# Preparing the second FFN's weights in step with the first FFN, and partly inside the second

## The chip, the cores and the metric

One core of one Trainium2 chip runs the kernel alone. The metric is the time of one execution on the device in microseconds (us). Engines: PE (TensorE, matmuls), DVE (VectorE), ACT (ScalarE), POOL (GpSimd); SP issues every DMA.

## What is computed

```python
# attention: batch 4, 8 heads, 576 tokens, head size 64, causal window of 128, a linear bias per head
x = attention(q, k, v)                       # 2304 tokens x 512
h = x @ w_in                                 # first FFN, 512 -> 2048
x = (h * sigmoid(1.702 * h)) @ w_out         # 2048 -> 512
g = x @ w_gate                               # second FFN, 512 -> 1536
v = x @ w_val
out = (g * sigmoid(g) * v) @ w_out           # 1536 -> 512, with a w_out of its own
```

All inputs are fp32. The second FFN's three weights arrive in DRAM as 64-bit words.

## The kernel before

**Tiling.** The 18 tiles of 128 tokens are split into five blocks of 4, 2, 4, 4 and 4 tiles (0 to 4). A *step* of the first FFN is one pair (block, 128 of the 2048 hidden columns): `h_steps` does 12 matmuls into a PSUM bank `hp`, ACT's `th<-hp` (tanh), DVE's `th<-th,hp`, ACT's `gh<-th` and DVE's `gl<-th,gh` (the high and the low part of the activation). `y_part` then adds 12 matmuls from `gh` and `gl` into four `y` banks. `y_part` runs two steps behind `h_part` (`AHEAD`). There are 80 steps in the order: block 0, steps 0 to 7; block 1; block 0's other eight (its *second half*); blocks 2, 3 and 4. The eight PSUM banks are one ring, so a late reader of a bank holds up the PE, which runs its instructions in order, as every engine does.

**Attention** of blocks 2, 3 and 4 is put between the steps of the blocks ahead of them: block 2's lies beside block 1 and block 0's second half, block 3's beside block 2, block 4's beside block 3. Nothing of attention lies beside block 4. It uses banks `sb` (scores), `pt` (transposes) and `xb` (values). At the end of a block the four `y` banks are evicted through one SBUF buffer `yt` to DRAM; block 0's second half first loads its earlier sum (`part`), into one of the two `th` buffers.

**Preparation of the second FFN's weights.** It works in *units*. A unit loads `raw` (512 KB), turns the words into fp32 `cs` (ACT `cs<-raw`, then three DVE operations, the last `cs<-cs,raw`), and splits that into a high part (ACT) and a low part (POOL), which SP writes to a scratch in DRAM. 24 units are for gate and value (G, V): they also make four sums `cs<-cs` on DVE, and their parts are `wa`, `wa` and `wb`. 12 units are for the output weight (O), with the part `wo`. The generators `prepare_gv` and `prepare_o` yield after each piece, 8 pieces for a G or V unit and 5 for an O unit; `advance` traces the next pieces. Before, `PACE` traces 6 pieces in each step from block 2 on, whatever is left of G and V ahead of block 4, and the O units in block 4.

**What sets the order.** The hand-written `PLAN` covers the start only. Behind it a scheduler orders all that is traced, at compile time: an instruction stands on its engine's queue where its inputs and buffers are ready by the scheduler's reckoning, so work that is traced late may stand early.

**Second FFN.** Three superblocks of six tiles, six weight pairs each: 18 turns `q`. A turn is 14 products of 6 matmuls (banks `sx`, `sy`, `sz`), four gates, and six output parts. Its inputs `ya` are built by `y_steps` (ACT and POOL), its weights `wg` and `wo` are loaded from the scratch each turn.

Of the kernel before, what the change touches and what calls it, by code (L numbers as in the profile page):

```python
# [16 lines left out]
P = 128  # L17
# [6 lines left out]

PACE = 3, 3

O_SLOTS = 4

SUPER = 6
# [44 lines left out]
def attention_two_ffn(ctx: ExitStack, tc: tile.TileContext, q, k, v, w_in, w_out, w_gate, w_val, w_out2, yscr, wscr, woscr, out):  # L74
# [149 lines left out]
    def flat(t):  # L224
        return t.bitcast(F32).rearrange("p s r c -> p (s r c)")

    def fetch_gv(pool, p, m, h):
        raw = pool.tile([P, 2, 2, P, 2], U32, tag="er", name="raw")
# [4 lines left out]
        return raw  # L233

    def prepare_gv(pool, raw, fetch_next, p, m, h):
# [24 lines left out]
        nc.sync.dma_start(out=at[:, 2048 + h * 768 : 2048 + (h + 1) * 768], in_=flat(wb))  # L260
        yield

    def prepare_o(pool, tag, f):
        raw = pool.tile([P, 512, 2], U32, tag=tag(), name="raw")
        nc.sync.dma_start(
            out=raw.rearrange("p c w -> p (c w)"), in_=w_out2[f * P : (f + 1) * P, :].bitcast(U32)
        )
        yield
        cs = cvp.tile([P, 8, P], F32, tag="cv", name="cs")
        yield from fraction(raw, cs)  # L270
        t = pool.tile([P, 1, 2, 512], F32R, tag=tag(), name="wo")
        halves(t, slice(0, 1), cs.rearrange("p s c -> p (s c)")[:, :512].unsqueeze(1))
        nc.sync.dma_start(out=woscr[f // 2][:, f % 2 * 1024 : (f % 2 + 1) * 1024], in_=flat(t))
        yield
# [277 lines left out]


    xs = {}
    ys = {}
    gs = {}

    def h_steps(j, f):
# [17 lines left out]
        gl = gp.tile([P, TMAX * P], F32R, tag="gl", name="gl")  # L576
        nc.scalar.activation(out=gh[:, :m], in_=th[:, :m], func=AF.Copy)  # L577
        yield
        nc.vector.tensor_tensor(out=gl[:, :m], in0=th[:, :m], in1=gh[:, :m].bitcast(F32), op=ALU.subtract)  # L579
        gs[j, f] = (gh, gl)  # L580
# [43 lines left out]
    def y_steps(s, tile_of):  # L624
# [15 lines left out]
        def minus(out_, a, b):  # L640
            nc.gpsimd.tensor_tensor(out=out_, in0=a, in1=b, op=ALU.subtract)

# [47 lines left out]
    def gv_steps(q):  # L690
# [212 lines left out]
    bctx = ExitStack()  # L903
    gv_todo = [(p, m, h) for p in range(NP2) for m in "GV" for h in range(2)]
    o_todo = list(range(NF2))

    def gv_work():
        raws = []

        def fetch_next():  # L910
            if len(raws) < len(gv_todo):
                raws.append(fetch_gv(att, *gv_todo[len(raws)]))

        fetch_next()
        yield
        for i, u in enumerate(gv_todo):
            yield from prepare_gv(att, raws[i], fetch_next, *u)

    turn = [0]

    def o_tag():
        turn[0] += 1
        return f"w{(turn[0] - 1) % O_SLOTS}"

    def o_work():
        for f in o_todo:
            yield from prepare_o(wpool, o_tag, f)

    gv_work, o_work = gv_work(), o_work()

    def advance(work, n):
        for _ in range(n):
            next(work, None)

    for idx, (j, f) in enumerate(seq):
# [4 lines left out]
        if j < 2:  # L940
# [17 lines left out]
        if j >= 2:  # L958
            advance(gv_work, PACE[1])
        if j == na - 1:  # L960
            if f % 2:
                next(first, None)
            if f >= O_SLOTS + 2:
                advance(o_work, 6)
    for i in range(len(seq) - AHEAD, len(seq)):
# [9 lines left out]
    for q in range(NQ):  # L975
# [71 lines left out]
```

## Time and profile before

| | |
|---|---|
| median of 3 runs | 961.38 us (961.23 to 965.03) |
| profiled execution | 959.06 us |
| its span | 957.3 us |
| PE busy | 925.3 us (97%) |
| DVE, ACT, POOL busy | 594.1, 423.7, 340.0 us |

The span is the time from the first to the last instruction of the profiled execution, 1.8 us less than its own time. A busy PE is not a PE at its peak, because the end of a matmul is modelled; starts are exact.

### The profile page before, as it was taken

How to read it: one execution, taken by the hardware profiler on the slowest of the kernel's cores; microseconds unless marked ns; L12 is line 12 of the kernel's file. 1: busy time of each engine (PE TensorE's matmuls, PEld its weight loads, DVE VectorE, ACT ScalarE, POOL GpSimd, SP SyncE). 2: the span in 40 equal slices, each digit the busy share in tenths (PEclk: the TensorE clock that was granted, in tenths of full speed). 3: DMA queues.
4: the chain of work that ended last, by engine and by line, in shares of the span. 5: the costliest groups of instructions: out<-in, count | busy, mean ns of one | idle time of the engine just before them, and what ended most of it. 6: DMA issues, size and time to landing. Idle time of an engine off the chain costs nothing.

```text
span 957.3 us, 15271 instructions
## 1 busy us (share of the span) xinstructions
PE 925.3 (97%) x5464; PEld 791.9 (83%) x5464; DVE 594.1 (62%) x1369; ACT 423.7 (44%) x968; POOL 340.0 (36%) x410
## 2 busy tenths in 40 slices
PE   7799999988999999999999999999999999999998
PEld 5477897776777777788887899999999999999997
DVE  7997898877777775433477474556534444535455
ACT  5664566655555454433345353234343333242331
POOL 4734007654466343313534461117511111111121
PEclk8899999999999999999999999999999999999999
DMA  9953204667556551010669385665775667766641
GB/s 335 346 210 124 76 2 156 217 227 248 209 183 229 202 213 52 15 50 1 198 206 360 123 301 201 210 219 202 263 243 205 212 215 245 252 213 208 216 166 66
DMA packets 62476, 182.40 MB, mean 191 GB/s; under 512 B 6080, under 2 KB 28096, under 8 KB 55488
## 3 DMA queue, kind: packets, MB, share of 16 engines
q1 hardware_dynamic: 62400, 181.43, 54.7%
q8 instruction: 43, 0.70, 0.3%
q14 instruction: 33, 0.27, 0.1%
HBM read 142.61 MB, written 38.80 MB: 189 GB/s over the span
## 4 chain that ended last, share of the span: by engine, by line
PE 61%; DVE 14%; DMA 10%; ACT 5%; issue 5%; POOL 4%; SPq 1%; DVEq 0%; POOLq 0%; ACTq 0%
PE o L751 16%; PE sx L681 15%; PE sz L681 8%; PE sy L681 4%; DMA raw<-in_moe_w_out 3%; PE y L549 3%; PE y L550 3%; PE y L551 3%; PE hp L549 2%; PE hp L551 2%; PE hp L550 2%; DVE cs L215 2%; DVE raw L211 2%; DMA wraw<-in_moe_w_out 2%; DMA y_scratch<-yt 2%
## 5 line engine op out<-in xcount | busy, mean ns | idle before, releaser
L715 POOL TENSOR_TENSOR p<-th,p 128x384 fp32r<-128x384 f32 x72 | 74.0, 1028 | 282.1 <-PE sz L681 147.8
L681 PE MATMUL sx<-ya,wg 128*128 128x384 f32 x864 | 173.3, 336 | 0.7 <-ACT pc L697 0.7
L751 PE MATMUL o<-wo,p 128*128 128x512 f32 x648 | 159.6, 391 | 0.0
L681 PEld LDWEIGHTS sx<-ya,wg 128*128 128x128 f32 x864 | 153.2, 188 | 6.5 <-ACT pc L697 1.0
L751 PEld LDWEIGHTS o<-wo,p 128*128 128x128 f32 x648 | 120.7, 188 | 21.3
L549 PE MATMUL hp<-xh,wt 128*128 128x512 f32 (+1 forms) x320 | 122.4, 382 | 4.7 <-DVE th L571 3.2
L550 PE MATMUL y<-gl,wt 128*128 128x512 f32 (+1 forms) x320 | 117.6, 373 | 2.3 <-DVE gl L579 2.3
L551 PE MATMUL hp<-xh,wt 128*128 128x512 f32 (+1 forms) x320 | 118.6, 371 | 0.0
L550 PE MATMUL hp<-xl,wt 128*128 128x512 f32 (+1 forms) x320 | 118.4, 370 | 0.0
L551 PE MATMUL y<-gh,wt 128*128 128x512 f32 (+1 forms) x320 | 117.2, 372 | 0.0
L549 PE MATMUL y<-gh,wt 128*128 128x512 f32 (+1 forms) x320 | 112.1, 381 | 4.8 <-DVE yt L611 2.9
L409 POOL TENSOR_SCALAR prob<-prob,stat 128x128 f32<-128x128 f32 x144 | 68.5, 495 | 128.4 <-DVE sb L319 56.8
L760 DVE SCALAR_TENSOR_TENSOR acc<-o,acc 128x512 f32<-128x512 f32 x90 | 61.9, 689 | 46.0 <-PE o L751 44.1
L681 PE MATMUL sz<-ya,wg 128*128 128x384 f32 x432 | 84.1, 335 | 0.0
L579 DVE TENSOR_TENSOR gl<-th,gh 128x512 fp32r<-128x512 f32 (+1 forms) x80 | 61.7, 776 | 32.8 <-ACT gh L577 32.8
L702 DVE TENSOR_TENSOR c<-sy,pc 128x384 f32<-128x384 f32 x36 | 20.1, 557 | 92.1 <-PE sy L681 92.1
L549 PEld LDWEIGHTS hp<-xh,wt 128*128 128x128 f32 x320 | 60.7, 190 | 19.5 <-DVE th L571 4.6
L681 PEld LDWEIGHTS sz<-ya,wg 128*128 128x128 f32 x432 | 75.8, 188 | 0.1
L549 PEld LDWEIGHTS y<-gh,wt 128*128 128x128 f32 x320 | 57.4, 189 | 19.6 <-DVE yt L611 3.3
L714 ACT ACTIVATE p<-th 128x384 fp32r<-128x384 f32 x72 | 37.5, 520 | 79.2 <-DVE th L712 79.2
L550 PEld LDWEIGHTS y<-gl,wt 128*128 128x128 f32 x320 | 60.8, 190 | 13.5 <-DVE gl L579 3.5
L551 PEld LDWEIGHTS y<-gh,wt 128*128 128x128 f32 x320 | 60.6, 189 | 11.2 <-issue 0.8
(90 smaller groups left out, 1524.7 us busy)
## 6 DMA issues: line engine op xcount, KB each, us to landing
wg<-w_scratch SPq DMA_DIRECT2D x36, 1024.0 KB, 6.6
wg<-w_scratch SPq DMA_DIRECT2D x36, 768.0 KB, 5.4
wo<-wo_scratch SPq DMA_DIRECT2D x18, 1024.0 KB, 7.0
w_scratch<-wa SPq DMA_DIRECT2D x24, 512.0 KB, 2.8
w_scratch<-wb SPq DMA_DIRECT2D x24, 384.0 KB, 2.9
wraw<-in_moe_w_in SPq DMA_DIRECT2D x16, 512.0 KB, 7.4
wraw<-in_moe_w_out SPq DMA_DIRECT2D x16, 512.0 KB, 8.6
raw<-in_moe_w_gate SPq DMA_DIRECT2D x24, 256.0 KB, 3.5
```

The costliest lines, as they stand in the source:

```text
L211: nc.vector.scalar_tensor_tensor(out=low, in0=low, scalar=29, in1=high, op0=ALU.logical_shift_right, op1=ALU.bitwise_or)
L409: (nc.vector if (j, hp, g) in NORM_ON_VECTOR else nc.gpsimd).tensor_scalar(out=prob[:, x], in0=prob[:, x], scalar1=stat[:, 3, x : x + 1], ...
L549: nc.tensor.matmul(out=out_ap, lhsT=whi, rhs=xhi, start=start, stop=False)
L550: nc.tensor.matmul(out=out_ap, lhsT=whi, rhs=xlo, start=False, stop=False)
L551: nc.tensor.matmul(out=out_ap, lhsT=wlo, rhs=xhi, start=False, stop=stop)
L579: nc.vector.tensor_tensor(out=gl[:, :m], in0=th[:, :m], in1=gh[:, :m].bitcast(F32), op=ALU.subtract)
L681: nc.tensor.matmul(out=bank_[:, :HT], lhsT=w[:, kk, at, a, :], rhs=y[:, b, kk, :], start=start and kk == 0 and n == 0, stop=kk == 1 and n ...
L702: nc.vector.tensor_tensor(out=t, in0=b[:, :HT], in1=kept[m, k], op=ALU.add)
L714: nc.scalar.activation(out=ph[:, 0, at], in_=th, func=AF.Copy)
L715: nc.gpsimd.tensor_tensor(out=ph[:, 1, at], in0=th, in1=ph[:, 0, at].bitcast(F32), op=ALU.subtract)
L751: nc.tensor.matmul(out=o, lhsT=ph[:, a, c], rhs=w[:, f, b, :], start=f == 0 and n == 0, stop=f == 1 and n == 2)
L760: nc.vector.scalar_tensor_tensor(out=acc, in0=o, scalar=0.5, in1=acc, op0=ALU.mult, op1=ALU.add)
```

## The change

Three things change. All 36 units go into one list ordered by weight pair, O units 2.5 pairs later, with the next unit's `raw` always loaded one unit ahead; the pace is 3.6 pieces a step in blocks 2 and 3, 6.8 in block 4 up to its step 13, and 0.7 for each product of the second FFN from product 6 of turn 0 on, until the list is done. Each piece's instructions are tied, in order, behind the last traced `gh` and `gl` (in the second FFN, behind the last `keep_copy` and `add`). The attention's buffers are closed at step 6 of block 4 and not at its step 0, and the first superblock's `y_steps` move there, with their four subtractions on DVE and not on POOL.

```diff
-PACE = 3, 3
+CLOSE = 6
+PACE = {2: 1.8, 3: 1.8, 4: 3.4}
+PAUSE = 13
+PACE_LATE = 0.7
 O_SLOTS = 4
+LATER = 2.5
...
+    def prepare(slot, raw, fetch_next, unit):
+
+        m, p, h = unit
         cs = cvp.tile([P, 8, P], F32, tag="cv", name="cs")
-        yield from fraction(raw.rearrange("p f a c w -> p (f a c) w"), cs)
+        yield from fraction(raw, cs)
         fetch_next()
+        if m == "O":
+            pool, tag = slot()
+            t = pool.tile([P, 1, 2, 512], F32R, tag=tag, name="wo")
+            halves(t, slice(0, 1), cs.rearrange("p s c -> p (s c)")[:, :512].unsqueeze(1))
+            nc.sync.dma_start(out=woscr[p][:, h * 1024 : (h + 1) * 1024], in_=flat(t))
+            yield
+            return
...
-            nc.gpsimd.tensor_tensor(out=out_, in0=a, in1=b, op=ALU.subtract)
+            (nc.gpsimd if s else nc.vector).tensor_tensor(out=out_, in0=a, in1=b, op=ALU.subtract)
...
+    todo = [(m, p, h) for p in range(NP2) for m in "GVO" for h in range(2)]
+    todo.sort(key=lambda u: u[1] + (LATER if u[0] == "O" else 0))
+    closed, turn = [], [0]
+
+    def slot():
+        if not closed:
+            return att, "er"
+        turn[0] += 1
+        return wpool, f"w{(turn[0] - 1) % O_SLOTS}"
...
+    def advance(n):
+        owed[0] += n
+        while owed[0] >= 1:
+            owed[0] -= 1
+            with ExitStack() as after:
+                for ins in marks.values():
+                    after.enter_context(tc.issue_after(ins))
+                next(work, None)
...
-        if (j, f) == (na - 1, 0):
-            advance(gv_work, 1000)
+        if (j, f) == (na - 1, CLOSE):
+            closed.append(True)
             attx.close()
...
-        if j >= 2:
-            advance(gv_work, PACE[0])
+        if (j, f) < (na - 1, PAUSE):
+            advance(PACE.get(j, 0))
...
         for n, (m, i) in enumerate(gv_steps(q)):
-            advance(o_work, 1)
+            if q or n > 5:
+                advance(PACE_LATE)
```

DVE in block 0's second half, between the `gl` of the 26th step and the next. Before:

```order
L579 TENSOR_TENSOR gl<-th,gh 128x512
L215 SCALAR_TENSOR_TENSOR cs<-cs,raw 128x512
L247 TENSOR_TENSOR cs<-cs 128x128 x3
L571 SCALAR_TENSOR_TENSOR th<-th,hp 128x512
L247 TENSOR_TENSOR cs<-cs 128x128
L545 TENSOR_TENSOR xb<-xb,half 128x512
L209 TENSOR_SCALAR raw<-raw 128x512
L211 SCALAR_TENSOR_TENSOR raw<-raw 128x512
L538 TENSOR_TENSOR xl<-xb,xh 128x512
L215 SCALAR_TENSOR_TENSOR cs<-cs,raw 128x512
```

The same place in the changed kernel:

```order
L592 TENSOR_TENSOR gl<-th,gh 128x512
L584 SCALAR_TENSOR_TENSOR th<-th,hp 128x512
L557 TENSOR_TENSOR xb<-xb,half 128x512
L550 TENSOR_TENSOR xl<-xb,xh 128x512
L592 TENSOR_TENSOR gl<-th,gh 128x512
```

The preparation has left this stretch. Counted by `cs<-cs,raw` on DVE's queue, units stand as follows: before block 2, 8 before and 0 now; block 2, 15 and 7; block 3, 1 and 8; block 4, 12 (all O) and 12 (8 G and V, 4 O); second FFN, 0 and 9 (3 G and V, 6 O).

SP's queue at the end of block 0's second half, where `part` is loaded and `yt` written. Before:

```order
L232 DMA raw<-in_moe_w_val 128x2x256 x2
L610 DMA part<-y_scratch 128x512
L256 DMA w_scratch<-wa 128x1024
L618 DMA y_scratch<-yt 128x512
L610 DMA part<-y_scratch 128x512
L260 DMA w_scratch<-wb 128x768
L610 DMA part<-y_scratch 128x512
```

Now:

```order
L311 DMA vr<-in_v 128x320 x4
L624 DMA part<-y_scratch 128x512
L632 DMA y_scratch<-yt 128x512
L624 DMA part<-y_scratch 128x512 x2
L308 DMA qr<-in_q 128x512
```

The unit's transfers no longer stand between the `part` loads.

ACT in turn 2 of the second FFN, whose copies `pc` and gates (`th`, `p`) stand here. Before:

```order
L697 ACTIVATE pc<-sx 128x384
L697 ACTIVATE pc<-sz 128x384
L697 ACTIVATE pc<-sx 128x384
L697 ACTIVATE pc<-sz 128x384
L710 ACTIVATE th_6088<-c_6067 128x384
L697 ACTIVATE pc<-sx 128x384 x2
L714 ACTIVATE p_6022<-th_6088 128x384
```

Now:

```order
L711 ACTIVATE pc<-sx 128x384
L229 ACTIVATE wo<-cs 128x512
L711 ACTIVATE pc<-sz 128x384
L216 ACTIVATE cs<-raw 128x512
L724 ACTIVATE th_6039<-c_6014 128x384
L711 ACTIVATE pc<-sx 128x384 x2
L216 ACTIVATE cs<-raw 128x512
L229 ACTIVATE wo<-cs 128x512
L728 ACTIVATE p_5961<-th_6039 128x384
```

Two O units' `cs<-raw` stand between the turn's copies, with one gate step and two copies between them.

## Rows read from the trace of the kernel before

**Rows 1.** Busy time of each engine in six stretches of the span.

```profile
core 0: us, PE busy (x) PEld busy (x) DVE busy (x) ACT busy (x) POOL busy (x), PEclk, DMA share, GB/s
161.20:226.30 65.10, 60.71 (x450) 47.07 (x451) 51.27 (x154) 39.49 (x104) 37.38 (x57) 0.97 0.63 217
226.30:348.60 122.30, 116.01 (x758) 89.68 (x758) 92.66 (x267) 64.58 (x170) 63.25 (x90) 0.99 0.62 213
348.60:452.60 104.00, 102.71 (x683) 80.44 (x682) 46.87 (x150) 43.64 (x112) 32.04 (x55) 1.00 0.15 49
452.60:536.60 84.00, 82.20 (x362) 67.40 (x361) 53.59 (x68) 37.56 (x63) 39.02 (x24) 1.00 0.69 238
541.00:655.00 114.00, 113.34 (x605) 106.76 (x604) 58.55 (x92) 44.79 (x90) 36.31 (x29) 1.00 0.64 222
655.00:940.00 285.00, 285.00 (x1498) 266.26 (x1497) 142.66 (x241) 95.74 (x193) 71.17 (x61) 1.00 0.63 216
```

**Rows 2.** The same stretches, line L549 alone (a third of a step's matmuls).

```profile
161.20:226.30 65.10, 28.04 (x68) 13.15 (x68) 0.97 0.63 217
226.30:348.60 122.30, 52.17 (x130) 24.54 (x130) 0.99 0.62 213
348.60:452.60 104.00, 48.73 (x121) 22.70 (x121) 1.00 0.15 49
```

**Rows 3.** The same, tile `sb` alone: PE, PEld and DVE.

```profile
161.20:226.30 65.10, 3.31 (x64) 2.06 (x64) 9.29 (x44) 0.97 0.63 217
226.30:348.60 122.30, 8.77 (x144) 5.13 (x144) 16.51 (x74) 0.99 0.62 213
348.60:452.60 104.00, 6.99 (x96) 4.08 (x96) 13.21 (x62) 1.00 0.15 49
```

**Rows 4.** The same, tile `xb` alone: PE, PEld, DVE and ACT.

```profile
161.20:226.30 65.10, 5.27 (x160) 4.21 (x160) 5.51 (x8) 4.71 (x8) 0.97 0.63 217
348.60:452.60 104.00, 7.06 (x192) 6.35 (x192) 5.57 (x8) 4.79 (x8) 1.00 0.15 49
```

**Rows 5.** The same, line L215 alone: DVE's `cs<-cs,raw`, one for each unit.

```profile
161.20:226.30 65.10, 5.36 (x8) 0.97 0.63 217
226.30:348.60 122.30, 9.71 (x15) 0.99 0.62 213
452.60:536.60 84.00, 13.40 (x12) 1.00 0.69 238
```

**Rows 6.** ACT in order of time, a step's `th<-hp` behind a unit's part.

```profile
191.45 0.42 ACT L221 ACTIVATE wa<-cs 128x256 fp32r<-128x256 f32 x1 [0.77 <-DVE cs L215]
193.40 0.58 ACT L569 ACTIVATE th<-hp 128x512 f32<-128x512 f32 x1
```

**Rows 7.** PE in order of time: the last `hp` matmul, and the next.

```profile
189.82 0.40 PE L551 MATMUL hp<-xh,wt 128*128 128x512 f32 x1
...
194.76 0.80 PE L549 MATMUL hp<-xh,wt 128*128 128x512 f32 x1 [2.58 <-DVE th L571]
```

**Rows 8.** PE's waits in the whole span: in total, times, longest.

```profile
PE y L549 <- DVE yt L611: 2.9, 1, 2.9
PE y L550 <- DVE gl L579: 2.3, 4, 0.9
...
PE y L549 <- ACT yt L615: 1.1, 1, 1.1
```

**Rows 9.** DVE in order of time: the first `yt` of block 0's second half.

```profile
230.24 0.69 DVE L611 SCALAR_TENSOR_TENSOR yt<-y,part 128x512 f32<-128x512 f32 x1 [1.55 <-DMA part<-y_scratch]
```

**Rows 10.** Tile `raw`: its transfers, from issue to landing.

```profile
DMA to landing us min/median/max: 2.9/3.6/6.5
```

**Rows 11.** DVE's `gl` in block 3, without and with POOL's `ya` beside it.

```profile
441.69 0.69 DVE L579 TENSOR_TENSOR gl<-th,gh 128x512 fp32r<-128x512 f32 x1 [2.06 <-ACT gh L577]
...
447.23 2.24 DVE L579 TENSOR_TENSOR gl<-th,gh 128x512 fp32r<-128x512 f32 x1 [2.06 <-ACT gh L577]
...
445.26 3.65 POOL L637 TENSOR_TENSOR ya<-yr,ya 128x768 fp32r<-128x768 f32 x2 [20.34 <-ACT ya L636]
```

More of the change, by code (lines that the diff above doesn't have):

```diff
@@ L225, in flat, with fetch @@
         return t.bitcast(F32).rearrange("p s r c -> p (s r c)")
-    def fetch_gv(pool, p, m, h):
-        raw = pool.tile([P, 2, 2, P, 2], U32, tag="er", name="raw")
+    def fetch(slot, unit):
+        m, p, h = unit
+        pool, tag = slot()
+        if m == "O":
+            raw = pool.tile([P, 512, 2], U32, tag=tag, name="raw")
+            src = w_out2[(2 * p + h) * P : (2 * p + h + 1) * P, :].bitcast(U32)
+            nc.sync.dma_start(out=raw.rearrange("p c w -> p (c w)"), in_=src)
+            return raw
+        raw = pool.tile([P, 2, 2, P, 2], U32, tag=tag, name="raw")
         w = w_gate if m == "G" else w_val
@@ L232, in fetch_gv @@
             nc.sync.dma_start(out=raw[:, f].rearrange("p a c w -> p a (c w)"), in_=src)
-        return raw
-    def prepare_gv(pool, raw, fetch_next, p, m, h):
+        return raw.rearrange("p f a c w -> p (f a c) w")
+    def prepare(slot, raw, fetch_next, unit):
+        m, p, h = unit
         cs = cvp.tile([P, 8, P], F32, tag="cv", name="cs")
-        yield from fraction(raw.rearrange("p f a c w -> p (f a c) w"), cs)
+        yield from fraction(raw, cs)
         fetch_next()
+        if m == "O":
+            pool, tag = slot()
+            t = pool.tile([P, 1, 2, 512], F32R, tag=tag, name="wo")
[3 more added lines that the diff above has]
+            return
         a11, a12, a21, a22, s4, s3, s1, s2 = (cs[:, i] for i in range(8))
@@ L260, in prepare_gv @@
         nc.sync.dma_start(out=at[:, 2048 + h * 768 : 2048 + (h + 1) * 768], in_=flat(wb))
[L261 to L273, printed above, removed]
         yield
@@ L551, in three @@
         nc.tensor.matmul(out=out_ap, lhsT=wlo, rhs=xhi, start=False, stop=stop)
+    marks = {}
     xs = {}
@@ L576, in h_steps @@
         gl = gp.tile([P, TMAX * P], F32R, tag="gl", name="gl")
-        nc.scalar.activation(out=gh[:, :m], in_=th[:, :m], func=AF.Copy)
+        a = nc.scalar.activation(out=gh[:, :m], in_=th[:, :m], func=AF.Copy)
         yield
-        nc.vector.tensor_tensor(out=gl[:, :m], in0=th[:, :m], in1=gh[:, :m].bitcast(F32), op=ALU.subtract)
+        d = nc.vector.tensor_tensor(out=gl[:, :m], in0=th[:, :m], in1=gh[:, :m].bitcast(F32), op=ALU.subtract)
+        marks["a"], marks["d"] = a.ins, d.ins
         gs[j, f] = (gh, gl)
@@ L696, in keep_copy @@
             t = pp.tile([P, HT], F32, tag="pc", name="pc", bufs=5)
-            nc.scalar.activation(out=t, in_=b[:, :HT], func=AF.Copy)
+            marks["a"] = nc.scalar.activation(out=t, in_=b[:, :HT], func=AF.Copy).ins
             kept[m, i] = t
@@ L701, in add @@
             t = pp.tile([P, HT], F32, tag="c2", name="c2", bufs=4)
-            nc.vector.tensor_tensor(out=t, in0=b[:, :HT], in1=kept[m, k], op=ALU.add)
+            marks["d"] = nc.vector.tensor_tensor(out=t, in0=b[:, :HT], in1=kept[m, k], op=ALU.add).ins
             c[m, i] = t
@@ L903, in attention_two_ffn, with preparation @@
     bctx = ExitStack()
-    gv_todo = [(p, m, h) for p in range(NP2) for m in "GV" for h in range(2)]
-    o_todo = list(range(NF2))
-    def gv_work():
+    todo = [(m, p, h) for p in range(NP2) for m in "GVO" for h in range(2)]
[6 more added lines that the diff above has]
+        return wpool, f"w{(turn[0] - 1) % O_SLOTS}"
+    def preparation():
         raws = []
         def fetch_next():
-            if len(raws) < len(gv_todo):
-                raws.append(fetch_gv(att, *gv_todo[len(raws)]))
+            if len(raws) < len(todo):
+                raws.append(fetch(slot, todo[len(raws)]))
         fetch_next()
         yield
[L916 to L933, printed above, removed]
+        for i, u in enumerate(todo):
+            yield from prepare(slot, raws[i], fetch_next, u)
+    work, owed = preparation(), [0.0]
+    def advance(n):
[6 more added lines that the diff above has]
+                next(work, None)
     for idx, (j, f) in enumerate(seq):
@@ L957, in attention_two_ffn @@
         run(2 * idx + 1)
[L958 to L964, printed above, removed]
+        if (j, f) < (na - 1, PAUSE):
+            advance(PACE.get(j, 0))
+        if j == na - 1 and f > CLOSE and f % 2:
+            next(first, None)
     for i in range(len(seq) - AHEAD, len(seq)):
```

3 lines of the change are left out of this document (2 added, 1 removed).

## The prediction, made before the changed kernel ran

> **What bounds the kernel now.** I read first the busy time by stretch. I cut the span where DVE's `gl` of a block's steps begin, so that the stretches are block 0's second half (65.1 us), block 2 (122.3), block 3 (104.0) and block 4 (84.0), then the first five turns of the second FFN and the rest [rows 1]. In the last stretch the PE is busy for 285.00 of 285 us, at the full granted clock: there the time is the PE's, and other engines' work is free as long as it isn't late. In block 2 the PE is busy for 116.0 of 122.3 us, while DVE is busy for 76% of it. In block 3, whose attention is of the same kind but which holds almost no units, DVE is busy for 45%.
>
> The cut is DVE's, and the PE stands now further ahead of it, now less, so the stretches don't hold the same matmuls; I take the first FFN's out by their count. Block 4 has no attention: 82.20 us for 362 matmuls is 0.227 us each [rows 1], or 0.681 us for each matmul of L549 with its two partners. That leaves for attention and stalls [rows 1, 2]:
>
> - block 0's second half: 65.1 − 68 × 0.681 = 18.8 us
> - block 2: 122.3 − 130 × 0.681 = 33.8 us
> - block 3: 104.0 − 121 × 0.681 = 21.6 us
>
> Block 2 also holds 48 more `sb` matmuls than block 3 [rows 3]; at 6.99/96 = 0.073 us each these are 3.5 us. So block 2 lost 33.8 − 21.6 − 3.5 = 8.7 us that block 3 didn't. Block 0's second half holds 64 of 96 `sb` matmuls and 160 of 192 `xb` matmuls [rows 3, 4]: by the one share it should take 14.4 us, by the other 18.0. I take the middle, 16.2, so it lost 2.6 us (0.8 to 4.4). What differs is the units: 8, 15 and 12 of them by their `cs<-cs,raw` in block 0's second half, block 2 and block 4 [rows 5], and one in block 3 by the order.
>
> How a unit costs PE time is seen in the order of time at 190 us. The last `hp` matmul starts at 189.82, so `hp` is done about 190.2 [rows 7]. ACT could take `th<-hp` then, but `wa<-cs` of a unit stands ahead of it and waits 0.77 us for DVE's `cs<-cs,raw`; `th<-hp` starts at 193.40 [rows 6]. The PE waits 2.58 us for the bank [rows 7], and the clock that the rows grant falls to 0.97 over this stretch [rows 1], which is 2.0 us of it. The waits are thus a matter of queues: a unit's piece in front of a step's piece.
>
> **Block 0's second half: −2.6 us.** The order shows no unit left there. All that its units cost comes back: 0.8 to 4.4 us.
>
> **Block 2's end of block 0: −1.5 us.** The `y` banks of block 0 leave one after another through `part`. The PE waited 2.9 us for `yt`, once [rows 8]; the first `yt` itself waited 1.55 us for `part` [rows 9]. The clock row of 0.99 is 1.2 us of block 2's 122.3 [rows 1]. Block 3 waits 1.1 us for its own `yt` [rows 8], so 2.9 + 1.2 − 1.1 = 3.0 us of the 8.7 are this chain's. In the changed queue of SP no unit's transfer stands between the `part` loads, and less is in flight beside them. But `part` still takes a `th` buffer, and still lands before `yt`. I take half: bounds 0 and −3.0 us.
>
> **Block 2: −4.3 us.** The other 8.7 − 3.0 = 5.7 us belong to 15 units: 0.38 us each. Now 7 units stand there. What one costs when fewer crowd is bounded by 0.38 above, and by block 4 below: 12 units beside steps without attention cost two waits for `gl` of 0.9 us [rows 8], 0.15 us each. Attention is still there, but at half the rate a unit's piece meets a step's piece less often; I take 0.2, so 1.4 us stay. Bounds: −3.0 (0.38 each) and −5.7 (none).
>
> **Block 3: +1.6 us.** Eight units where one was; at 0.2 us 1.6. Bounds 0 and +3.0. It has room: 15 units raised DVE's share in block 2 by 31 points over block 3's 45%, so 8 units raise block 3's to some 62 to 65%.
>
> **Block 4: 0.** Twelve units before and now; eight have four more operations on DVE, but they begin at the block's first step and not at its seventh. The `ya` splits move a few steps later, and four subtractions of 128x768 go from POOL to DVE; no row has them on DVE, so I bound them by `gl` (128x512, 0.69 us [rows 11]) below and by twice that above: 3 to 6 us in all, beside 84 us in which DVE is busy for 53.6. Bounds ±1.8 us, the two waits for `gl` gone or doubled.
>
> **Second FFN: +0.7 us.** Nine units stand in the first turns, where none was. The first 114 us already carry such work before (POOL busy for 32%, against 25% behind it, with `ya` of the next superblock) and the PE lost 114.0 − 113.3 = 0.7 us there [rows 1]. I take once more that. Bounds: 0, and the rival below.
>
> The Trainium skill (GPSIMD Engine Reference, Specifications) says that POOL shares its SBUF interfaces with VectorE and contends with DVE instructions that have two inputs in SBUF. The trace agrees: `gl` took 2.24 us beside POOL's `ya`, and 0.69 us one step earlier with POOL idle [rows 11]. This speaks against the change in the second FFN, where every unit brings POOL one to three parts beside the gates; by 1.55 us for each of nine units it would be 14 us of DVE time. DVE has half of its time free there, so I add nothing for it.
>
> **Sum.** −2.6 − 1.5 − 4.3 + 1.6 + 0 + 0.7 = −6.1 us. The profiled execution took 959.06 us (1.8 us of it outside the span), so 953.0. The median of the three runs is 961.38, higher by a factor of 1.0024; on its scale the forecast is 955 us. With every bound at its best the sum is −4.4 − 3.0 − 5.7 + 0 − 1.8 + 0 = −14.9, or 946.5 on the median's scale; at its worst without the rival below −0.8 − 0 − 3.0 + 3.0 + 1.8 + 0.7 = +1.7, or 963.
>
> **Rivals.** *The cost moves with the units.* If a unit costs 0.38 us wherever attention is, 15 units in blocks 2 and 3 cost what they did in block 2 alone: −2.6 − 3.0 + 3.0 + 0.7 = −1.9 with the `yt` chain unchanged, 957.2, and 959.5 on the median's scale. For it: the tie sets only the earliest place, and in the new order units' parts still stand ahead of `th<-hp` now and then. Against it: 8.7 us in one block and almost nothing in the next is more than in proportion to DVE's 76% and 45%.
>
> *The second FFN waits for `raw`.* ACT and DVE take their instructions in order; behind a `cs<-raw` whose transfer is late stand the copies `pc` and the sums that free the banks for the PE. For two O units in a row, the second `raw` is issued only when the first has gone through three DVE operations, some 2 us, and it lands 2.9 to 6.5 us later [rows 10]. The new order puts a gate step and two copies between the two `cs<-raw`; at 285.00/1498 = 0.19 us for a matmul [rows 1] a product is 1.14 us, so that is about 3.4 us. With the median landing of 3.6 us `cs<-raw` is 2 + 3.6 − 3.4 = 2.2 us late, with the longest 5.1. A bank is wanted again one to four products later (1.1 to 4.6 us). If it is one, six O units cost 6 × (2.2 − 1.1) = 7 us at the median landing and 24 at the longest; I take 3.3 us late, the middle of 2.2 and 4.4: 6 × 2.2 = 13 us. The sum is then −6.1 + 13 = +7, 966 and 968.5 on the median's scale. It decides from a landing of about 4.5 us on, if nothing but one product lies between. Against it: the scheduler can put work of the next product in front, and in the first five turns the PE lost only 0.7 us in all while the weights' loads and `ya` went on [rows 1].
>
> The Trainium skill (DMA: Bandwidth & Descriptors, Issuing engines are not separate DMA queues) has all transfers share the same 16 DMA engines and interleave. The share is 0.63 to 0.64 in both stretches of the second FFN [rows 1], so units there lengthen `raw` and the weights' loads; it feeds this rival and has no price of its own here.
>
> *The units cost nothing once tied.* If the tie keeps pieces out of the steps' way altogether, blocks 0, 2 and 3 give −2.6 − 3.0 − 5.7 = −11.3, plus 0.7: 948.5, and 951 on the median's scale.
>
> **Chances.** Three runs of one kernel differ by up to 0.4%, so 0.5% (4.8 us) is about what can be told from no change. Forecast, between 952 and 958: 0.48. Free once tied, below 952: 0.21. Cost moves along, 958 to 963: 0.18. Waiting for `raw`, above 963: 0.13. A gain of over 0.5% is below 956.6: all of the second case and most of the first, 0.62. No change 0.26, slower 0.12 (above 966.2, nearly all of the last case). Leaving out the last case and the best few, the range is 946 to 963; the forecast alone, with its bounds, is 950 to 959.
>
> **What would show it.** Right: no unit's operation before block 2, PEclk 1.00 in block 0's second half, no wait of the PE for `th` there; the remainder of block 2 by the reckoning above near 28 us and of block 3 near 23; DVE busy about 65% in both; the first five turns within 1 us of 114. Wrong: block 3's remainder rises by as much as block 2's falls; or `sx`, `sy` or `sz` waits for `c` or `pc` while ACT's `cs<-raw` waits for a transfer; or the 2.9 us wait for `yt` stands as before.

## The result and the profile after

The changed kernel takes 948.47 us (median of four runs, 945.89 to 949.73), the kernel before 961.31 us on the same chip (four runs). The ratio is 0.9858 with an interval of 0.9821 to 0.9894, a gain of about 13 us. The profiled execution took 945.89 us and its span is 944.2. That is inside the range of 946 to 963, but below the forecast's 955 and below the 950 to 959 that the forecast alone spans: the gain is about twice the 6.1 us that the sum gave.

Busy time of each engine after, in stretches cut as in [rows 1] where DVE's `gl` of a block's steps begin, columns as there:

```profile
159.90:214.30 54.40, 54.40 (x459) 43.57 (x453) 27.24 (x100) 25.97 (x74) 13.98 (x28) 1.00 0.18 55
214.30:322.40 108.10, 108.10 (x738) 85.51 (x737) 68.70 (x216) 52.58 (x141) 43.68 (x69) 1.00 0.42 145
322.40:431.30 108.90, 108.90 (x720) 85.37 (x719) 68.08 (x197) 52.55 (x135) 44.53 (x68) 1.00 0.36 124
431.30:521.80 90.50, 86.48 (x376) 69.81 (x375) 65.81 (x102) 42.25 (x78) 40.93 (x35) 1.00 0.74 261
521.80:640.00 118.20, 116.10 (x619) 109.10 (x619) 77.70 (x131) 54.53 (x111) 50.22 (x43) 1.00 0.83 295
```

Line L561 alone (L549 before), which holds a third of a step's matmuls, as in [rows 2]:

```profile
159.90:214.30 54.40, 24.75 (x62) 11.65 (x62) 1.00 0.18 55
214.30:322.40 108.10, 51.22 (x128) 24.16 (x129) 1.00 0.42 145
322.40:431.30 108.90, 51.02 (x128) 23.91 (x128) 1.00 0.36 124
```

In the first three stretches the PE is now busy without a gap, at the full granted clock. DVE is busy for 64% of block 2 and 63% of block 3, as the prediction had it. With 0.681 us for each L561 matmul as in the prediction, 12.2 us remain in block 0's second half (18.8 before), 20.9 in block 2 (33.8) and 21.7 in block 3 (21.6). Block 4 goes the other way: 90.5 − 123 × 0.681 = 6.7 us remain, where the 84.0 us before were its matmuls and 1.6 us. DVE's busy time and the DMA share grow in the two stretches that follow block 3.

These stretches do not hold the same matmuls on both sides. For the comparison I therefore cut at the PE itself, at the first `hp` matmul of a step, which is the same instruction in every kernel: steps 24, 32, 48, 64 and 79, counted in the order in which steps are issued. PE rows in order of time (start, duration), before:

```profile
154.07 0.48 PE L549 MATMUL hp<-xh,wt 128*128 128x512 f32 x1
...
214.89 0.39 PE L549 MATMUL hp<-xh,wt 128*128 128x512 f32 x1
...
335.02 0.40 PE L549 MATMUL hp<-xh,wt 128*128 128x512 f32 x1
...
446.36 0.39 PE L549 MATMUL hp<-xh,wt 128*128 128x512 f32 x1
...
530.37 0.39 PE L549 MATMUL hp<-xh,wt 128*128 128x512 f32 x1
```

The same five matmuls after:

```profile
154.67 0.39 PE L561 MATMUL hp<-xh,wt 128*128 128x512 f32 x1
...
206.71 0.39 PE L561 MATMUL hp<-xh,wt 128*128 128x512 f32 x1
...
314.57 0.40 PE L561 MATMUL hp<-xh,wt 128*128 128x512 f32 x1
...
424.98 0.39 PE L561 MATMUL hp<-xh,wt 128*128 128x512 f32 x1
...
511.70 0.39 PE L561 MATMUL hp<-xh,wt 128*128 128x512 f32 x1
```

Their differences give the table by stage, in us; the last stage runs to the end of the span and holds block 4's last step and the second FFN. The rows for the experiments below are read in the same way. "Units" are counted by their `cs<-cs,raw` in the instruction order of DVE, in five places: ahead of block 2, in blocks 2, 3 and 4, and in the second FFN.

```
kernel          start  0 (2nd half)  block 2  block 3  block 4  rest   span   units
before          154.1      60.8       120.1    111.3     84.0   426.9  957.3  8/15/1/12/0
after           154.7      52.0       107.9    110.4     86.7   432.5  944.2  0/7/8/12/9
after, again    155.6      52.0       107.9    110.4     87.5   434.4  947.8  0/7/8/12/9
untied          155.4      59.3       125.4    108.3     86.1   435.7  970.2  8/14/0/11/3
before_tied     156.0      52.0       111.4    110.0     81.6   429.5  940.5  0/11/12/11/2
the same again  154.9      52.0       111.3    110.1     81.6   432.1  942.0  0/11/12/11/2
tie_act         155.3      52.0       109.0    109.6     81.6   430.2  937.8  0/11/12/12/1
tie_dve         156.1      52.0       112.9    110.5     81.6   430.1  943.3  0/11/12/11/2
tied_dense      155.3      52.0       112.4    114.5     85.1   428.6  948.0  0/11/15/10/0
mix             155.0      52.0       109.3    109.4     87.1   433.8  946.6  0/8/10/12/6
close1          155.0      52.0       107.9    110.4     86.8   431.8  943.9  0/7/8/12/9
sub_pool        155.1      52.0       107.9    110.4     87.9   437.1  950.4  0/7/8/13/8
bt_pace5        154.7      52.0       111.6    109.9     89.1   432.1  949.4  0/9/10/14/3
no_units        210.5      52.2       107.8    108.3     90.7   426.9  996.4  none
```

From before to after: −8.8 in block 0's second half, −12.2 in block 2, −0.9 in block 3, then +2.7 in block 4 and +5.6 in the rest. The gain up to block 3 is 21.9 us, and 8.3 of it are given back behind it (0.6 more at the start makes the span's −13.1).

The PE's waits show both halves. From 147 to 432 us the view of the PE's waits, which before named `yt`, `th` and others [rows 7, 8], has no row at all after. From 432 to 700 us it has three (total, times, longest):

```profile
PE y L562 <- DVE gl L592: 3.8, 3, 1.8
PE sx L695 <- DMA wg<-w_scratch: 2.1, 1, 2.1
PE sx L695 <- DVE c L716: 1.6, 2, 1.4
```

At the place of [rows 6], where `th<-hp` stood behind a unit's `wa<-cs`, ACT now reads:

```profile
185.22 0.60 ACT L582 ACTIVATE th<-hp 128x512 f32<-128x512 f32 x1 [3.58 <-PE hp L563]
```

ACT has no unit's operation in this stretch, and it waits for the PE where the PE waited for it. The chain of [rows 9] is still there, but holds up nobody. The first `yt` on DVE after:

```profile
217.79 0.69 DVE L625 SCALAR_TENSOR_TENSOR yt<-y,part 128x512 f32<-128x512 f32 x1 [0.31 <-DMA part<-y_scratch]
```

No wait of the PE for `yt` is left. The chain begins earlier: SP issues the first `part` load just after a `gl` has ended (at 227.07 before and 214.96 after); that is at 227.09 before, 12.2 us after the PE began step 32, and at 215.00 now, 8.3 us after it.

### The profile page after: what moved, and what is told of

It reads as the page before. It is cut to its first block, busy times and chain, and to the rows that moved or that the text cites. A ratio compares the mean times of both kernels' runs of the same rounds, so it can differ in the third digit from the quotient of the medians.

```text
span 944.2 us, 15242 instructions
## 1 busy us (share of the span) xinstructions
PE 919.8 (97%) x5464; PEld 787.9 (83%) x5464; DVE 598.2 (63%) x1373; ACT 422.0 (45%) x968; POOL 333.8 (35%) x406
## 4 chain that ended last, share of the span: by engine, by line
PE 74%; DMA 9%; DVE 9%; POOL 3%; issue 2%; ACT 2%; SPq 0%; POOLq 0%; DVEq 0%; ACTq 0%
PE sx L695 13%; PE o L765 13%; PE sz L695 7%; PE hp L561 5%; PE hp L563 5%; PE hp L562 5%; PE y L563 5%; PE y L562 5%; PE y L561 5%; PE sy L695 3%; PE sb L361 2%; PE xb L514 2%; DMA wraw<-in_moe_w_out 2%; PE pt L453 2%; POOL ya L651 1%
## 5 line engine op out<-in xcount | busy, mean ns | idle before, releaser
L729 POOL TENSOR_TENSOR p<-th,p 128x384 fp32r<-128x384 f32 x72 | 75.9, 1054 | 240.4 <-ACT p L728 115.9
L561 PE MATMUL hp<-xh,wt 128*128 128x512 f32 (+1 forms) x320 | 121.0, 378 | 0.5 <-DVE th L584 0.4
L561 PE MATMUL y<-gh,wt 128*128 128x512 f32 (+1 forms) x320 | 111.3, 377 | 0.1
L592 DVE TENSOR_TENSOR gl<-th,gh 128x512 fp32r<-128x512 f32 (+1 forms) x80 | 52.7, 663 | 42.8 <-ACT gh L590 42.2
L590 ACT ACTIVATE gh<-th 128x512 fp32r<-128x512 f32 (+1 forms) x80 | 46.6, 585 | 62.6 <-PE y L563 42.9
L230 POOL TENSOR_TENSOR wa<-cs,wa 128x256 fp32r<-128x256 f32 x48 | 41.5, 872 | 93.5 <-ACT wa L229 88.9
L584 DVE SCALAR_TENSOR_TENSOR th<-th,hp 128x512 f32<-128x512 f32 (+1 forms) x80 | 49.8, 629 | 37.3 <-ACT th L582 36.6
L402 ACT ACTIVATE prob<-prob,stat 128x128 f32<-128x128 f32 x144 | 56.2, 393 | 36.9 <-DVE stat L386 36.7
```

The lines of the kernel that those rows point to most:

```text
L402: nc.scalar.activation(out=prob[:, x], in_=prob[:, x], func=AF.Exp, bias=stat[:, 0, x : x + 1], scale=-1.0, accum_out=stat[:, 1, x : x + 1],)
L561: nc.tensor.matmul(out=out_ap, lhsT=whi, rhs=xhi, start=start, stop=False)
L584: nc.vector.scalar_tensor_tensor(out=th[:, :m], in0=th[:, :m], scalar=1.0, in1=hp[:, :m], op0=ALU.add, op1=ALU.mult)
L590: a = nc.scalar.activation(out=gh[:, :m], in_=th[:, :m], func=AF.Copy)
L592: d = nc.vector.tensor_tensor(out=gl[:, :m], in0=th[:, :m], in1=gh[:, :m].bitcast(F32), op=ALU.subtract)
L729: nc.gpsimd.tensor_tensor(out=ph[:, 1, at], in0=th, in1=ph[:, 0, at].bitcast(F32), op=ALU.subtract)
```

## The experiments

Two theories were open after the result. The first: the tie alone brings the gain, and the new paces, the new list and the place of the O units give part of it back. The rival: a unit's piece meets a step's piece less often because fewer units stand in block 2, so the paces bring the gain and the tie adds little. Ratios are to the kernel before, timed beside it on the same chip; behind each is its 95% interval.

**The change without its tie (untied).**

```diff
-            with ExitStack() as after:
-                for ins in marks.values():
-                    after.enter_context(tc.issue_after(ins))
-                next(work, None)
+            next(work, None)
```

> The changed kernel with its list, paces, closing step and subtractions, but without the tie behind the last gh and gl. By the order the scheduler then puts 8 units ahead of block 2 again and 14 into block 2, 11 in block 4, 3 in the second FFN. Theory (the place in the queues costs: a unit in front of a step's piece beside attention): block 0's second half and block 2 lose what they lost before, so 956 to 960 us, less the 2 to 5 us that the second FFN no longer loses. Rival (the lower pace is what helps): as the changed kernel, 946 to 950.

Measured: 970.68 us, 1.0078 (1.0049 to 1.0108). It is slower than both expectations and slower than the kernel before. Without the tie the scheduler pulls the units forward again: 8 ahead of block 2, 14 in it, none in block 3. The PE's waits from 147 to 432 us, the three largest:

```profile
PE y L561 <- DVE yt L625: 4.1, 2, 2.8
PE hp L561 <- ACT pf L476: 3.9, 2, 2.3
PE hp L561 <- DVE th L584: 2.6, 1, 2.6
```

Where the third and the second arise, ACT and PE read in order of time:

```profile
192.75 0.42 ACT L229 ACTIVATE wa<-cs 128x256 fp32r<-128x256 f32 x1 [0.77 <-DVE cs L223]
194.71 0.58 ACT L582 ACTIVATE th<-hp 128x512 f32<-128x512 f32 x1
196.07 0.50 PE L561 MATMUL hp<-xh,wt 128*128 128x512 f32 x1 [2.59 <-DVE th L584]
...
269.75 0.66 ACT L216 ACTIVATE cs<-raw 128x512 f32<-128x512 f32 x1 [2.73 <-DMA raw<-in_moe_w_gate]
270.31 0.58 ACT L476 ACTIVATE pf<-pt 128x512 f32<-128x512 f32 x1
270.95 0.50 PE L561 MATMUL hp<-xh,wt 128*128 128x512 f32 x1 [2.30 <-ACT pf L476]
```

The first three lines are the picture of [rows 6, 7] again: on ACT a unit's `wa<-cs` waits for DVE, and the step's `th<-hp` stands behind it. In the next three a unit's `cs<-raw` waits for its transfer, with the attention's `pf` queued behind it and the PE behind `pf`. The wait of 2.8 us for `yt` is the chain of [rows 9]: the `part` load, issued at 232.52, landed at 235.87, and `yt` began at 235.97. All this comes back although the pace asks for 7 units in block 2 and not for 14. The point of the program at which a unit is written does not hold it there; the tie does.

**The kernel before with the tie and nothing else (before_tied, run twice).**

```diff
+    marks = {}
...
-        nc.scalar.activation(out=gh[:, :m], in_=th[:, :m], func=AF.Copy)
+        a = nc.scalar.activation(out=gh[:, :m], in_=th[:, :m], func=AF.Copy)
...
-        nc.vector.tensor_tensor(out=gl[:, :m], in0=th[:, :m], in1=gh[:, :m].bitcast(F32), op=ALU.subtract)
+        d = nc.vector.tensor_tensor(out=gl[:, :m], in0=th[:, :m], in1=gh[:, :m].bitcast(F32), op=ALU.subtract)
+        marks["a"], marks["d"] = a.ins, d.ins
...
-            next(work, None)
+            with ExitStack() as after:
+                for ins in marks.values():
+                    after.enter_context(tc.issue_after(ins))
+                next(work, None)
```

> The kernel before with one edit: each piece is tied behind the last traced gh and gl; paces, lists, subtractions and closing step as before. By the order 0, 11, 12 and 11 units now stand ahead of block 2, in block 2, block 3 and block 4, and 2 in the second FFN. Theory (place in the queues): most of the gain comes with this edit alone, 945 to 950 us, since block 0's second half is clear and blocks 2 and 3 hold fewer than 15. Rival (lower pace): 11 and 12 units cost 0.38 us each beside attention, and block 0's second half gives back 7: 953 to 957.

Measured: 944.07 us, 0.9803 (0.9771 to 0.9836). The first theory holds, and the rival falls. Block 0's second half takes 52.0 us, as after; block 2, now with 11 units, 111.4. The PE's waits from 147 to 432 us:

```profile
PE xb L502 <- DVE stat L374: 1.0, 1, 1.0
PE hp L549 <- DVE th L572: 1.0, 2, 0.7
```

To see whether the tie alone is faster than the whole change, both were timed again on one chip, with six runs each.

> The tie alone once more, in five rounds beside the changed kernel: 0.978 to 0.983 of the time before, and less than the changed kernel by 3 to 6 us. If paces, list, second FFN and subtractions are worth something of their own, it is the slower of the two.

> The changed kernel itself, beside the tie alone on the same chip: 0.984 to 0.988 of the time before.

Measured: 943.51 us, 0.9793 (0.9766 to 0.9821) for the tie alone, and 949.43 us, 0.9856 (0.9827 to 0.9884) for the whole change. The intervals do not touch: what the change does besides the tie costs about 6 us. By stages it wins 3.5 us in block 2 (107.9 against 111.4) and loses 5 to 6 in block 4 and 2 to 3 in the rest.

**What a unit costs where it stands (no_units).** The transfers of the units stay, their arithmetic goes (its core):

```diff
-        cs = cvp.tile([P, 8, P], F32, tag="cv", name="cs")
-        yield from fraction(raw, cs)
         fetch_next()
+        for _ in range(3):
+            yield
+        bits = filler.unsqueeze(1).to_broadcast([P, 4, 256])
...
-            halves(t, slice(0, 1), cs.rearrange("p s c -> p (s c)")[:, :512].unsqueeze(1))
-            nc.sync.dma_start(out=woscr[p][:, h * 1024 : (h + 1) * 1024], in_=flat(t))
+            nc.sync.dma_start(out=woscr[p][:, h * 1024 : (h + 1) * 1024].rearrange("p (a c) -> p a c", a=4), in_=bits)
```

> The changed kernel with the units' arithmetic left out: the scratch is filled from a small constant, so the second FFN multiplies by 0.01 everywhere; all the units' transfers then fall into the first 150 us. It gives each stage its time without units. Theory (tied units cost nothing beside attention): from step 32 to step 48 and from 48 to 64 the PE takes within 1 us of the changed kernel's 107.9 and 110.4, and what the changed kernel loses lies behind: block 4 82 us where it takes 86.7, the rest 427 to 428 where it takes 432.5. Rival (units still cost 0.2 us or more each beside attention): 1.5 to 3 us less in each of blocks 2 and 3.

Measured: 998.67 us, 1.0359, which says nothing of the units: their writes to the scratch crowd into the first 143 us, and the start takes 210.5 us instead of 155. Against the expectation the loads of `raw` do not all run there: the last of them lie between 498 and 535 us. So block 4 can't serve as a floor either; ACT's `ya` waited 12.64 and 6.59 us in it, by the rows for `raw`. The three stages between, in which no unit's transfer is left, and the rest are of use: 52.2, 107.8, 108.3 and 426.9 us. (untied, with no unit in block 3, takes 108.3 there too.) So in the changed kernel 7 units in block 2 cost 0.1 us together, 8 in block 3 cost 2.1 us, and with 9 in it the rest is longer by 5.6.

**More units while attention runs, none in the second FFN (tied_dense).**

```diff
-PACE = {2: 1.8, 3: 1.8, 4: 3.4}
+PACE = {2: 3.0, 3: 3.0, 4: 3.4}
```

> The changed kernel with 6 pieces a step in blocks 2 and 3 (as before) and not 3.6: 11 and 15 units there, 10 in block 4, none in the second FFN. Theory (tied units cost nothing beside attention): the second FFN's and block 4's losses of some 8 us shrink to 3, so 940 to 944 us. Rival (density beside attention costs, 0.38 us a unit): 11 more units there cost 4 us, which eats the gain: 946 to 950.

Measured: 950.73 us, 0.987 (0.9842 to 0.9898). The theory missed, and the time lies just above the rival's range. The rest is cheaper by 3.9 us with no unit in it (428.6), but 11 units in block 2 cost 4.6 us above the floor and 15 in block 3 cost 6.2. Tied units are free only while they are few: 7 in block 2 are, while 8 there cost 1.5 us (mix, below), 9 cost 3.8 (bt_pace5, below) and 11 cost 1.2 to 5.1 in the four kernels that have so many.

**The subtractions back on POOL (sub_pool).**

```diff
-            (nc.gpsimd if s else nc.vector).tensor_tensor(out=out_, in0=a, in1=b, op=ALU.subtract)
+            nc.gpsimd.tensor_tensor(out=out_, in0=a, in1=b, op=ALU.subtract)
```

> The changed kernel with the first superblock's four subtractions back on POOL. In the changed kernel's trace the PE waits 3.8 us for gl in block 4, and gl at 489.01 us stands behind a subtraction of 2.50 us. Theory (the subtractions on DVE make gl late): 1.5 to 3.5 us less, 945 to 947. Rival (gl is late through the units' eight fuller DVE operations and POOL's contention, whoever subtracts): the same within 1 us, or slower, since POOL has 8 us more to do.

Measured: 951.96 us, 0.9882 (0.985 to 0.9915), not faster than the whole change. The PE's largest wait from 432 to 700 us:

```profile
PE y L562 <- DVE gl L592: 5.8, 5, 2.4
```

The wait for `gl` grows from 3.8 to 5.8 us. So taking the subtractions off DVE does not cure the lateness of `gl` in block 4.

**The attention's buffers closed at step 1 of block 4, next to where it was before (close1), and paces between (mix).**

```diff
-CLOSE = 6
+CLOSE = 1
```

The second has this edit and one more:

```diff
-PACE = {2: 1.8, 3: 1.8, 4: 3.4}
+PACE = {2: 2.2, 3: 2.2, 4: 3.4}
```

> The changed kernel with the attention's buffers closed at step 1 of block 4 and not at step 6, so that y_steps run at its steps 3 to 9 and not at 7 to 13; units where they were (7, 8, 12, 9). Theory (the lateness of gl in block 4 comes from y_steps and units falling on the same steps, and pushes units into the second FFN's start): block 4 loses about 2 us less, 945 to 947. Rival (it is the 8 G and V units themselves, whatever stands beside them): as the changed kernel within 1 us, 947.5 to 949.5.

> As close1, with 4.4 pieces a step in blocks 2 and 3: 8 units in block 2, 10 in block 3, 12 in block 4 and 6 in the second FFN (all O). Theory (up to about ten tied units in a block are free beside attention, and each in the second FFN costs some 0.5 us): 1.5 us faster than close1, 943 to 946. Rival (units in the second FFN cost nothing of their own): as close1.

Measured: close1 945.25 us, 0.9807 (0.9773 to 0.9842); mix 949.56 us, 0.9863 (0.9823 to 0.9903). Block 4 stays at 86.8 and 87.1 us, so the place of the closing does not explain it. The median of close1 is in the range of its theory and below the changed kernel's, but not in the theory's way: the stages are the same as far as block 4, and the intervals overlap. The theory of mix missed: 6 units in the second FFN cost as much as 9 (433.8 against 431.8 in close1, 432.5 and 434.4).

**The tied kernel at a slower pace (bt_pace5):** before_tied with one line more.

```diff
-PACE = 3, 3
+PACE = 2, 3
```

> The kernel before with the tie alone, and 5 pieces a step and not 6: 9, 10 and 14 units in blocks 2, 3 and 4, 3 in the second FFN. With the tie alone at 6 it was 944.1, with 11 units in block 2 taking 111.4 us where 7 take 107.9. Theory (a tied unit is free up to eight or nine in a block): block 2 gains 2 to 3 us, and block 4 loses 1 to 2 with three more units: 941 to 944. Rival (block 4 is as full as it can be): 944 to 947.

Measured: 951.74 us, 0.9873 (0.9844 to 0.9901). Theory and rival both missed: with 9 units instead of 11 block 2 gains nothing (111.6), and block 4, with three more units, takes 7.5 us longer (89.1).

**The tie on one engine (tie_act, tie_dve):** before_tied with one of the two marks.

```diff
-        marks["a"], marks["d"] = a.ins, d.ins
+        marks["a"] = a.ins
```

```diff
-        marks["a"], marks["d"] = a.ins, d.ins
+        marks["d"] = d.ins
```

> As the kernel before with the tie, but tied on ACT alone, behind the last gh. By the order the units stand where both ties put them (0, 11, 12, 12, and 1 in the second FFN). Theory (the tie works by holding units back from the stretch ahead of block 2 and from crowding into it): one engine is enough, 942 to 947 us. Rival (the tie works by keeping each queue's pieces behind the step's piece): without DVE's part half of the gain goes, 950 to 955.

> The same with the tie on DVE alone, behind the last gl. Units by the order 0, 11, 12, 11, and 2 in the second FFN. Theory (held back): 942 to 947 us, block 0's second half 52 us from step 24 to 32. Rival (each queue): parts stand ahead of th on ACT again, 950 to 955.

Measured: tie_act 939.97 us, 0.9761 (0.9721 to 0.98); tie_dve 946.27 us, 0.9827 (0.9793 to 0.9861). One tie is enough, on either engine: the rival, that each queue needs a tie of its own (950 to 955), falls twice. On ACT alone it gives the shortest of all medians, below its theory's 942 to 947 too; its interval overlaps that of before_tied. In tie_act the PE waits once from 147 to 432 us,

```profile
PE hp L549 <- DVE th L572: 0.6, 1, 0.6
```

and block 2 with its 11 units takes 109.0 us.

## Why the prediction held, and where its sizes were off

**What held.** The mechanism: units' pieces in front of steps' pieces in the queues of ACT and DVE. No unit is left ahead of block 2, the clock is 1.00 there, the PE waits for no `th`, and DVE's shares came out as forecast. Without the tie the same waits come back (untied), and the tie alone removes them (before_tied). The rival that the cost moves along did not happen: eight units in block 3 cost 2.1 us above the floor, where 0.38 each would be 3.0, and seven in block 2 cost nothing. The case that happened is the rival *free once tied*, but only as far as block 3, and with the loss behind it that neither the forecast nor this rival had.

That the total fell inside the range is luck. Up to block 3 the sum has −6.8 us, −13.1 at its best, and −21.9 were measured; behind it the sum has +0.7, +2.5 at its worst without the rivals, and +8.3 were measured. The two misses, of opposite sign, offset each other in part. Of the signs named ahead, the remainders of blocks 2 and 3 came out at 20.9 and 21.7 where 28 and 23 stood, and from the first product of turn 0 to that of turn 5 the PE took 111.0 us (520.6 to 631.6), where before took 109.4 (538.5 to 647.9).

**Block 0's second half** was mis-sized: −2.6 forecast, −8.8 measured. The units' price there was taken as 18.8 us less 16.2, the middle between two shares of block 3's remainder. The remainder without units is 12.2 us by the same reckoning, and no_units shows the stage at 52.2 where before took 60.8. Block 3 was no clean yardstick: it held one unit, yet took 111.3 us against 108.3 in no_units, so 3 us above the floor went into what the prediction called the price of attention. The PE's waits name 1.3 of them.

**Block 2 and block 0's end** were mis-sized together: −4.3 and −1.5 forecast, −12.2 measured, all of it down to the floor (107.9 against 107.8). Two reasons. The 3.5 us taken off for more `sb` matmuls come from the cut at DVE. Cut at the PE, blocks 2 and 3 of the kernel before hold the same number (tile `sb` alone, as [rows 3]):

```profile
214.89:335.02 120.13, 7.88 (x128) 4.59 (x128) 16.28 (x72) 0.99 0.62 214
335.02:446.36 111.34, 8.76 (x128) 5.12 (x128) 15.14 (x72) 1.00 0.21 71
```

Nor do they show in the time: without units the sixteen steps of block 2 take 107.8 us and those of block 3 108.3. And the 0.2 us for a unit and the half of the `yt` chain that was to stay were both too high: seven tied units cost 0.1 us, and the PE waits for `yt` no more. What the trace of before showed as 0.38 us a unit was the price of a unit placed in front, not of a unit.

**Block 3:** +1.6 forecast, −0.9 measured, since the block had stood 3.0 us above its floor before. Against its floor the eight units cost 2.1 us, 0.26 each, near the 0.2 assumed. That they are dearer than in block 2 was not explained.

**Block 4:** 0 forecast with bounds of ±1.8, +2.7 measured. The PE's two long waits for `gl`, and DVE's side of them, engine by engine:

```profile
489.74 0.50 PE L562 MATMUL y<-gl,wt 128*128 128x512 f32 x1 [1.81 <-DVE gl L592]
503.15 0.50 PE L562 MATMUL y<-gl,wt 128*128 128x512 f32 x1 [1.60 <-DVE gl L592]
...
485.65 2.50 DVE L655 TENSOR_TENSOR yr<-yr 128x768 f32<-128x768 f32 x1
...
489.01 0.68 DVE L592 TENSOR_TENSOR gl<-th,gh 128x512 fp32r<-128x512 f32 x1
...
499.48 2.21 DVE L219 SCALAR_TENSOR_TENSOR raw<-raw 128x512 uint32<-128x512 uint32 x1
...
502.41 0.69 DVE L592 TENSOR_TENSOR gl<-th,gh 128x512 fp32r<-128x512 f32 x1
```

and beside it ACT and POOL:

```profile
485.82 0.63 ACT L590 ACTIVATE gh<-th 128x512 fp32r<-128x512 f32 x1
...
485.49 1.85 POOL L651 TENSOR_TENSOR ya<-yr,ya 128x768 fp32r<-128x768 f32 x1 [2.38 <-ACT ya L650]
...
499.12 2.03 POOL L651 TENSOR_TENSOR ya<-yr,ya 128x768 fp32r<-128x768 f32 x1
```

`gh` is done at 486.45 and `gl` starts at 489.01: it stands behind a subtraction that took 2.50 us beside POOL's `ya`, where the next such subtraction, at 491.46, took 0.95, and behind two of a unit's sums. At 499.48 it is a unit's operation that took 2.21 us beside POOL instead of 0.69, again with `gl` behind it. The contention that the prediction read from [rows 11], and for which it named the Trainium skill (GPSIMD Engine Reference, Specifications), was thus looked for in the wrong place: it does delay `gl`, in block 4. But it is not the whole cause, since with the subtractions on POOL the waits were longer. In all kernels with 10 or 11 O units and one G or V unit in block 4 the stage takes 81.6 us; with 8 G or V units and 4 O units 86.7, with 4 and 6 units 85.1 (tied_dense), and with 5 and 9 units 89.1. That a G or V unit is the dearer neighbour of the `ya` splits fits this, but was not isolated; the cause stays open.

**The second FFN:** +0.7 forecast, +5.6 measured, the largest miss of the terms that lose. The PE's waits there are 3.7 us, where before lost 0.7. The first is for the weights; DMA and PE in order of time:

```profile
531.41 6.64 DMA wg<-w_scratch
538.19 1.29 PE L695 MATMUL sx<-ya,wg 128*128 128x384 f32 x6 [2.10 <-DMA wg<-w_scratch]
```

The busy time around it, after:

```profile
520.00:548.00 28.00, 25.89 (x144) 24.64 (x143) 20.25 (x37) 15.71 (x34) 11.79 (x13) 1.00 0.94 337
```

Before, in the 28 us that answer to these:

```profile
538.00:566.00 28.00, 27.34 (x152) 26.21 (x151) 15.79 (x20) 13.86 (x27) 16.02 (x11) 1.00 0.58 199
```

In the second profile of the changed kernel the wait at this place is 2.96 us, and there too the PE goes on, at 540.70, just after the load has landed, at 540.56. The load that the PE waits for took 6.64 us here, where the same load before, issued at 548.74, took 5.59; and it was issued 1.3 us later, counted from the PE's start of step 79. The DMA share rises from 0.58 to 0.94: the `raw` and the scratch transfers of units now fall where the second FFN's first weights come in. The Trainium skill (DMA: Bandwidth & Descriptors, Issuing engines are not separate DMA queues) has all transfers interleave on the same engines; the trace agrees, and the prediction had given this no price.

The other wait, for `c`, arises at 650 us, behind the last unit, in turn 5. DVE, ACT and PE there:

```profile
637.11 0.56 DVE L716 TENSOR_TENSOR c<-sy,pc 128x384 f32<-128x384 f32 x1 [3.52 <-PE sy L695]
642.21 2.18 DVE L725 SCALAR_TENSOR_TENSOR th<-th,c 128x384 f32<-128x384 f32 x1 [4.54 <-POOL ya L651]
...
639.39 0.84 ACT L650 ACTIVATE ya<-yr 128x768 fp32r<-128x768 f32 x1 [2.90 <-POOL yr L655]
641.60 0.51 ACT L724 ACTIVATE th<-c 128x384 f32<-128x384 f32 x1
...
650.46 1.30 PE L695 MATMUL sx<-ya,wg 128*128 128x384 f32 x6 [1.38 <-DVE c L716]
```

A gate's `c` is done at 637.67, but on ACT two pieces of the next superblock's `ya` stand in front of the gate's `th<-c`, and the first waits 2.90 us for POOL. So `th<-c` starts 3.9 us late, DVE's gate operations behind it are late, and DVE comes late to the `c` that the PE waits for. Before, `th<-c` at this place in turn 5 started 0.1 us after its `c`:

```profile
654.06 0.52 ACT L710 ACTIVATE th<-c 128x384 f32<-128x384 f32 x1 [1.20 <-DVE c L702]
```

The contention of block 4 is here as well: DVE's gate operation takes 2.18 us beside POOL, where the same operation at 534.81 took 0.55. But it took 2.13 us before too, at 654.62, and no wait of the PE followed. So the loss is one of place in a queue once more, in a stretch that the units have already left; why the order of ACT changed there was not traced.

By turns the 5.6 us are 0.7 up to the first product of turn 0, 1.5 in turn 0, 3.0 in turns 5 and 6 and 0.3 elsewhere. The waits name 1.4 in turn 0 (2.1 less the 0.7 of before) and 1.6 in turns 5 and 6, so some 2.5 us have no wait with a name. Two profiles of the changed kernel differ by 1.9 us in this stage, and two of before_tied by 2.6.

The rival *the second FFN waits for `raw`* did not happen, though its condition came true: the six loads of `raw` for O units there landed after 6.8 us in the median, past the 4.5 from which it was to decide. What failed was its 3.4 us between issue and use. The loads were issued 12 to 22.5 us ahead of their `cs<-raw`, all but the last, at 592.87, and only that one was waited for; SP and ACT in order of time:

```profile
592.87 0.38 SPq L242 DMA_DIRECT2D raw<-in_moe_w_out  x1
...
599.50 0.68 ACT L216 ACTIVATE cs<-raw 128x512 f32<-128x512 f32 x1 [2.73 <-DMA raw<-in_moe_w_out]
```

The PE did not wait behind it.

**What stays open:** why 11 tied units in block 2 cost 3.6 us above the floor in before_tied and 5.1 in tie_dve, but 1.2 in tie_act; what besides the subtractions makes `gl` late in block 4; and why the rest is 2.6 to 5.2 us longer than before in the four profiles with only one or two units in it. The place of this last loss is known: it lies in turn 0, which takes 22.6 us in before_tied and 18.2 before, and the PE waits there, longest 2.36 us at 536.70, for ACT's `pc`, which stands behind a gate's `p`, whose two DVE operations took 1.97 and 2.10 us beside POOL's `ya`. No run had the changed kernel with its tie on ACT alone.

## What to carry to other kernels

Side work that a scheduler is free to pull forward is priced by where it lands in the queues, not by how much of it there is: 24 units up to block 3 cost 8.6 + 12.3 + 3.0 = 23.9 us above the floor in front of the steps' pieces (before), and 23 cost 3.6 + 1.7 = 5.3 us behind them (before_tied). An order tie to the instruction that paces the steps did this here in a few lines, while a new pace without it made the kernel slower; take the tie first, measure it by itself, and change the pace only after. A stage's price without the side work is best read from a kernel that leaves the side work out: a neighbouring stage that seemed free of it stood 3 us above its own floor, and a cut at another engine gave it 96 of its 128 `sb` matmuls; both mis-sized the terms that were measured against it.

## What the runs showed of the hardware

How contention between DVE and POOL works out in time. DVE operations with two inputs took far longer beside 128x768 operations on POOL: 2.18 us instead of 0.55 for 128x384, 2.21 instead of 0.69 for 128x512, 2.50 instead of 0.95 for 128x768, and a sum of 128x128 at 489.61 took 1.92 instead of 0.28. No factor fits these. What fits is that the operation is held until the POOL operation is over and then takes its own time: `ya` at 499.12 ends at 501.15, and 501.15 + 0.69 − 0.14 is 501.70, where `raw<-raw` ends by its row at 501.69; `ya` at 485.49 ends at 487.34, and 487.34 + 0.95 − 0.14 is the subtraction's end at 488.15. All 66 DVE operations of the changed kernel's trace that took over 0.25 us longer than others of their line and shape end so, 0.13 to 0.15 us ahead of that sum. `raw<-raw` with one input is among them (1.81 us instead of 0.42 at 479.60). The cost fell on whatever was queued behind.

And in the second FFN one load of `raw`, issued at 572.16 where the DMA share was 0.86 for 10 us, took 9.3 us to land, against 6.5 as the longest before [rows 10].
